# Moving two background W_down transfers to another phase and taking another seeded instruction order, in a one-core linear-attention and GeGLU block

## Chip, cores and metric

The kernel runs on one core of a Trainium2 chip. The metric is device time in microseconds (us) of that core; lower is better. A time is quoted as the median of the runs of one kernel with its lowest and highest run. All runs were fast, at a mean granted clock of 0.992 to 1.00 over the whole span.

The engines are called as the profile calls them: PE is TensorE (matmuls and transposes), PEld its weight loads, DVE VectorE, ACT ScalarE, POOL GpSimd, and SP the engine whose queue issues most loads.

## The reference

One transformer block with adaptive layer norm: linear attention, then a GeGLU feed-forward network. Shapes: x is 2048 x 1024, W_qkv 1024 x 3072, W_gate and W_up 1024 x 3584, W_down 3584 x 1024, w_mod 1024 x 6144; all bf16.

```python
mod = (silu(c) @ w_mod).reshape(1, 6, 1, -1)      # shifts, scales and gates
h = layernorm(x) * (1 + ca) + sa
q, k, v = split(h @ wqkv)                         # 32 heads of 32
pq, pk = phi(q), phi(k)                           # phi: t + 1 where t > 0, else exp(t); + 1e-6
kv = einsum('bhsd,bhse->bhde', pk, v)
z = einsum('bhsd->bhd', pk)
o = einsum('bhqd,bhde->bhqe', pq, kv) / (einsum('bhqd,bhd->bhq', pq, z) + 1e-6)
x = x + ga * (o @ wo)
h = layernorm(x) * (1 + cb) + sb
x = x + gb * ((gelu(h @ w_gate) * (h @ w_up)) @ w_down)
```

## The kernel before

Three features carry the argument. The first is how the order of instructions comes about. The kernel is not written in its final order: every call is recorded as an operation, with its predecessors, and a model of the engines then places all operations in time. PE keeps the recorded order; DVE, ACT, POOL and SP take, at each moment, the ready operation with the earliest due time. A backward sweep from the end sets the due times, a forward sweep places the operations, and this is repeated; the best forward sweep, by the model's own time, is issued. On the chip each queue then runs strictly in that order.

```python
class Plan:
    def order(self):
        best = None
        def forward(look):
            nonlocal best
            t = self.sweep(False, lambda o: (o.due, o.n), look)
            if best is None or t < best[0]:
                best = (t, sorted((op.start, op.n) for op in self.ops))
        for op in self.ops:
            op.due = op.n
        for i in range(2 * self.ROUNDS):                 # 32 rounds
            forward(i >= self.ROUNDS)
            old = [op.due for op in self.ops] if i else None
            for op in self.ops:
                op.due = op.start
            t = self.sweep(True, lambda o: (-o.due, -o.n))
            for op in self.ops:
                op.due = best[0] * (1 - op.done / max(t, best[0]))
                if old:
                    op.due += self.KEEP * (old[op.n] - op.due)
            # ... (pairs and chains keep their order)
        return [self.ops[n] for _, n in best[1]]
```

The second is a background job. The matmuls with W_down use sums of its quarters (a Strassen-like scheme). Part of these sums is made by DMA, DRAM to DRAM: a raw copy of a half of W_down into the scratch `ub`, then accumulating transfers onto it. Small marker copies on POOL hold each transfer back until PE has reached a certain instruction.

```python
def move(dst, src, add):
    gp.dma_start(out=dst, in_=src, **(dict(accum_op=ALU.add) if add else {}))

def paced_moves(seen_of, moves):
    plan.hold([op for op in plan.ops if op.eng == "PE"][-1])
    gp.tensor_copy(out=seen, in_=seen_of)                # the marker
    plan.hold(plan.ops[-1])
    for dst, src, add in moves:
        move(dst, src, add)
    plan.hold()

sums_copy = [(ub_scr[:, e], wd_v[1].rearrange("p (c e) n -> p e c n", e=2)[:, e], 0) for e in range(2)]
sums_add = [(flat[:, e, :, s, :], flat[:, f, :, t, :], 1)
            for e, s, f, t in ((0, 0, 0, 1), (0, 1, 1, 1), (1, 1, 0, 0), (1, 0, 1, 1))]
late_moves = {1: sums_copy[1:2], 3: sums_add[1:2], 5: sums_add[2:3], 7: sums_add[3:4]}

def gate_up(g):
    # ...
    for n in range(NU):                                  # units of gate/up
        # ...
        if g == 0 and n in late_moves:
            paced_moves(w["s1"][:, 0, 0, 0:1], late_moves[n])
```

The third is what the merge phase does at that time: it finishes the kv sums, makes the reciprocal denominators, writes them to DRAM and reads them back broadcast over partitions, so that DVE can multiply the queries.

```python
def merge_phase(stages):
    # ... loads of w_mod and Wo
    for i, stage in enumerate(stages):
        if i < NKB:
            kv_products(NG - 1, i)
        # ...
        if i == 5:
            den_sums(0, psN())                           # ACT: Ln, Exp; SP: write den to DRAM
        if i in (8, 10):
            den_mul(den_todo.pop(0))                     # SP: broadcast den back; DVE: multiply
        # ...

def start_phase():
    xs, loads = [], []
    for tt in range(TT):                                 # four x tiles
        xs.append(load_x(tt))
        # ...
    ca = ModRow(1, wm_ca, {0: loads[0], 2: loads[1], 4: loads[2], 6: loads[3]})   # four w_mod loads
    # ... per tile: two bn_stats, bn_aggr, rstd on ACT, normalise on DVE, eight transposes on PE
```

Of the kernel before, what the change touches and what calls it, by code (L numbers as in the profile page):

```python
# [3 lines left out]

# [19 lines left out]
class Plan:  # L24
# [115 lines left out]
    def cost(self, op, outs, ins):  # L140

        size = lambda a: math.prod(d[1] for d in a.ap[1:])
        n = max(size(a) for a in (outs if op.eng == "PE" else outs + ins))
        psum = any(a.tensor.name.startswith("psum") for a in outs + ins)
        wide = any(a.dtype == FP32 and size(a) > 8 for a in outs + ins)
        ptrs = sum(size(a) == 1 for a in ins)
        if op.eng == "PE":
            op.cost = n / 2.4 + 2.5
            op.lat = op.cost + 165
            if op.fn == "matmul" and outs[0].ap[0][1] <= 32:  # L150
                op.cost /= 3.5
        elif op.fn.startswith("dma"):
            a = outs[0]
            op.cost, op.bytes = 1000 if op.eng == "POOL" else 450, math.prod(d[1] for d in a.ap) * (4 if a.dtype == FP32 else 2)
            run = min(self.run(a) for a in outs + ins)
            if not any(a.tensor.name.startswith("mem") for a in outs + ins):
                op.bytes = int(op.bytes * self.GBPS * (12 + run / 27) / 16 / run * (2.3 if "accum_op" in op.kw else 1.6))
            op.load = a.tensor.name.startswith("mem")
            if op.fn == "dma_start_transpose":
                op.cost, op.bytes = self.transpose  # L160
            op.lat = op.cost
        elif op.eng == "ACT":
            op.cost = (55 if psum else 112) + n / 1.2 + 85 * ptrs
            op.lat = op.cost + 115
            f = op.kw.get("func")
            op.table = "g" if f == AF.Gelu_apprx_tanh else "e" if f in (AF.Exp, AF.Ln) else None
        elif op.eng == "POOL":
            op.cost = 500 if n <= 8 else 250 + n / 0.46
            op.lat = 1800 if n <= 8 else op.cost
        else:  # L170
            rate = 1.0
            if op.fn in ("tensor_scalar", "tensor_scalar_mul", "tensor_scalar_add", "tensor_copy") and not wide:
                rate = 1.0 if psum else 4.0
            elif op.fn == "tensor_tensor" and not wide:
                rate = 2.0
            op.cost = 69 + n / (0.96 * rate) + 61 * ptrs
            op.lat = op.cost + 83
# [9 lines left out]
    def sweep(self, back, key, look=False):  # L187
# [68 lines left out]
                    avail[o.eng].append(o)  # L256
        return max(op.done for op in ops)

    def order(self):


        best = None

        def forward(look):
            nonlocal best
            t = self.sweep(False, lambda o: (o.due, o.n), look)
            if best is None or t < best[0]:
                best = (t, sorted((op.start, op.n) for op in self.ops))

        for op in self.ops:  # L270
            op.due = op.n
        for i in range(2 * self.ROUNDS):
            forward(i >= self.ROUNDS)
            old = [op.due for op in self.ops] if i else None
            for op in self.ops:
                op.due = op.start
            t = self.sweep(True, lambda o: (-o.due, -o.n))
            for op in self.ops:
                op.due = best[0] * (1 - op.done / max(t, best[0]))
                if old:  # L280
                    op.due += self.KEEP * (old[op.n] - op.due)
            for a, b in [*zip(self.chain, self.chain[1:]), *self.pairs]:
                b.due = max(a.due, b.due)
        return [self.ops[n] for _, n in best[1]]

    def issue(self):
        with self.tc.manual_schedule():
# [9 lines left out]
def kernel(  # L297
# [45 lines left out]
    mem = mem_pool.tile([P, 103 * KB + KB // 2], BF16, name="mem", tag="mem")  # L343
# [51 lines left out]
    def at(off, shape, dt):  # L395
        return Ring(off, shape, dt, 1)()
# [76 lines left out]
    kvzacc = at(190, [KD, P + 1], FP32)  # L473
# [89 lines left out]
    def tt_op(out, a, b, op):  # L563
        ve.tensor_tensor(out=out, in0=a, in1=b, op=op)  # L564
# [414 lines left out]
    def kv_products(b, kb):  # L979
        glo, ghi = kb * GPB, min(KD, (kb + 1) * GPB)  # L980
        kvps = (psKV1 if b == 0 else psKV if b == 3 else QB)()[:, 0:GPB * (P + 1)].rearrange("p (g e) -> p g e", e=P + 1)
        for tl in range(TT):
            for g in range(glo, ghi):
                te.matmul(kvps[:, g - glo, :], lhsT=pks[b, tl // 2][:, tl % 2, g * P:(g + 1) * P],  # L984
                                 rhs=vta[:, tl][:, g, 0:P + 1], start=(tl == 0 and g == glo), stop=(tl == TT - 1),
                                 skip_group_check=True)
        src = kvps[:, 0:ghi - glo, :]
        if b == 0:
            ve.tensor_copy(out=kvzacc[:, glo:ghi, :], in_=src)
        else:  # L990
            tt_op(kvzacc[:, glo:ghi, :], src, kvzacc[:, glo:ghi, :], ALU.add)
# [19 lines left out]
    def den_mul(b):  # L1011
        plan.extra = 4000
        rden = rden_ring()
        plan.together(True)
        for j in range(P // DH):
            src = den_scr[b // 2][b % 2, j].rearrange("h x -> (h x)")
            sy.dma_start(out=rden[DH * j:DH * j + DH].rearrange("p g t -> p (g t)"),
                         in_=src[None, :].to_broadcast((DH, KD * TG)))
        plan.together(False)
        plan.extra = 0  # L1020
        for g in range(0, KD, 2):
            o = pqT[b][:, g:g + 2, :]
            tt_op(o, o, rden[:, g:g + 2, :], ALU.mult)
# [9 lines left out]
    def kv_diagonal():  # L1033
        gp.memset(zc, 0.0)
        for g in range(KD):
            ve.tensor_scalar_mul(out=zc[:, g, g % KH:KH * P // DH:KH], in0=maskbd[:, 0:P:DH], scalar1=kvzacc[:, g, P:P + 1])
        tt_op(KVbd, kvzacc[:, :, 0:P], maskbd[:, None, :].to_broadcast((P, KD, P)), ALU.mult)

    def kv_transposes():
        for half in range(2):  # L1040
            psk = psN(F16)[:, 0:NW].rearrange("p (g e) -> p g e", e=P)
            for g in range(4):
                te.transpose(psk[:, g, :], KVbd[:, half * 4 + g, :], ident)
            ve.tensor_copy(out=KVbdT[:, half * 4:half * 4 + 4, :], in_=psk)
# [3 lines left out]
    def move(dst, src, add):  # L1048
        gp.dma_start(out=dst, in_=src, **(dict(accum_op=ALU.add) if add else {}))  # L1049
# [13 lines left out]
    def paced_moves(seen_of, moves):  # L1063

        plan.hold([op for op in plan.ops if op.eng == "PE"][-1])
        gp.tensor_copy(out=seen, in_=seen_of)
# [5 lines that stand above are left out]
    def wd_moves(seen_of, n):  # L1072

        if wd_todo:
# [4 lines left out]
    sums_copy = [(ub_scr[:, e], wd_v[1].rearrange("p (c e) n -> p e c n", e=2)[:, e], 0) for e in range(2)]  # L1079
    flat = ub_scr.rearrange("p e c (j s n) -> p e (c j) s n", j=2, s=2)  # L1080
    sums_add = [(flat[:, e, :, s, :], flat[:, f, :, t, :], 1)
                for e, s, f, t in ((0, 0, 0, 1), (0, 1, 1, 1), (1, 1, 0, 0), (1, 0, 1, 1))]
    late_moves = {1: sums_copy[1:2], 3: sums_add[1:2], 5: sums_add[2:3], 7: sums_add[3:4]}

    def second_sum(name, f):

# [181 lines left out]
    def merge_phase(stages):  # L1268

        ms1 = ModSet(1, wm1_ring, psK)  # L1270
        sy.dma_start(out=Wo_sb, in_=A_wo.rearrange("(kd p) n -> p kd n", p=P))
        wp = list(range(KD))
        for i, stage in enumerate(stages):
            if i < NKB:
                kv_products(NG - 1, i)
            if i in (1, 3):
                for _ in range(KH):
                    ms1.step()
            if i == 3:
                kv_diagonal()  # L1280
            if i == 3 + 1:
                kv_transposes()
                ms1.columns()
                ms1.spread(0, garow, GA_SCALE)
                for g in range(KD):
                    tt_op(Wog[:, g, :], Wo_sb[:, g, :], garow, ALU.mult)
            if i == 5:
                den_sums(0, psN())
            if i in (8, 10):
                den_mul(den_todo.pop(0))  # L1290
            if i >= 6:
                wp_step(wp.pop(0))
            if i == 11:
                ms2 = ModSet(2, wm2_ring, psN)
            stage(())
        for g in wp:
            wp_step(g)
        return ms2
# [261 lines left out]
    def down_out(g):  # L1560
# [223 lines left out]
        run(*plain("t3", A22, c21_out(rest(1, 0)), False))  # L1784

    wo_phase(merge_phase(kvq_phase()))
    gate_up(0)
    down_out(0)
# [31 lines left out]
```

## Time and profile before

| | before |
|---|---|
| time, three runs before the prediction | 749.08 us (748.78 to 749.98) |
| span in the profile | 746.4 us |
| PE busy | 730.0 us (98%) |
| next busiest engine | DVE, 79% |
| PE lost beyond its pitch after 40 us | 7.27 us |
| PE lost in the start | about 10 us |

The stages in time are: start (0 to 45 us), k/v blocks (to 155), merge (to 210), output projection (to 245), gate/up 0 (to 415), down 0 (to 495), gate/up 1 (to 655), down 1. With PE at 98% a gain can come only from PE's gaps, so one reads what ended each gap. The prediction below counts these gaps by pitch, the distance of successive matmul starts in a steady stream.

A second measure is used after the result: because PE executes the same list in every kernel here (but for ten filler matmuls in two of them, which are left out), its instructions can be paired one to one between two traces, and the difference of their start times shows where one kernel runs ahead of or behind the other. I paired the weight loads, which are complete in number where a few matmul records are missing. The profiled run of before took 748.54 us.

### The profile page before, as it was taken

The numbers are of one execution on the slowest core, as the hardware profiler recorded it, in microseconds if no ns is written. First come the engines' busy times: TensorE is split into PE (matmuls) and PEld (weight loads), VectorE is DVE, ScalarE is ACT, GpSimd is POOL, SyncE is SP. The second block draws the span as 40 slices with busy tenths as digits, with TensorE's granted clock in tenths as the row PEclk, the third lists the DMA queues.
The fourth block names the chain that finished last, engine by engine and source line by source line (L and its number), as shares of the span: only waits on it lengthen the run. The fifth ranks groups of instructions, "written<-read, shape, count | busy, mean of one in ns | idle before, by whom it ended". The sixth has DMA issues, their size and how long they took to land.

```text
span 746.4 us, 11439 instructions
## 1 busy us (share of the span) xinstructions
PE 730.0 (98%) x4164; PEld 388.7 (52%) x4164; DVE 589.5 (79%) x1258; ACT 433.0 (58%) x757; POOL 95.8 (13%) x164
## 2 busy tenths in 40 slices
PE   5999999999999999999999999999999999999997
PEld 2444445444444455545454586545555555548664
DVE  6897997577786878777997888678888888888763
ACT  3665576669752768997876234027777777731000
POOL 2331245000001113342311000010000000000000
PEclk9999999999999999999999999999999999999999
DMA  8974479828899979899659799654131322399822
GB/s 298 322 212 132 152 182 163 299 101 258 245 290 257 364 253 261 259 318 227 187 191 237 210 281 314 206 183 132 60 114 57 112 73 98 110 276 302 278 104 71
DMA packets 151832, 152.79 MB, mean 205 GB/s; under 512 B 33824, under 2 KB 128544, under 8 KB 150496
## 3 DMA queue, kind: packets, MB, share of 16 engines
q1 hardware_dynamic: 128832, 122.44, 53.7%
q0 software_dynamic: 20592, 27.53, 15.6%
q10 hardware_dynamic: 2352, 2.10, 0.8%
q8 instruction: 32, 0.52, 0.3%
q14 instruction: 24, 0.20, 0.1%
HBM read 123.34 MB, written 36.04 MB: 214 GB/s over the span
## 4 chain that ended last, share of the span: by engine, by line
PE 84%; DVE 6%; ACT 5%; DMA 3%; issue 1%; SPq 1%; ACTq 0%; DVEq 0%
PE psum L1382 30%; PE psum L1588 13%; PE psum L1632 9%; PE psum L870 8%; PE psum L1393 7%; PE psum L1262 7%; PE psum L940 5%; DVE mem L564 5%; PE psum L969 4%; DMA mem<-in_A_wqkv_dram 2%; DMA mem<-in_w_mod_dram 1%; PE psum L984 1%; ACT mem L815 1%; DVE psum L564 1%; ACT psum L1436 1%
## 5 line engine op out<-in xcount | busy, mean ns | idle before, releaser
L564 DVE TENSOR_TENSOR mem<-mem 128x512 f16<-128x512 f16 (+8 forms) x669 | 307.8, 507 | 23.1 <-ACT mem L815 10.1
L1382 PE MATMUL psum<-mem 128*128 128x512 f16 x1248 | 299.1, 379 | 0.8 <-ACT psum L1436 0.5
L815 ACT ACTIVATE mem<-psum 128x256 f32<-128x256 f32 (+3 forms) x284 | 154.3, 562 | 119.9 <-PE psum L1382 45.1
L564 DVE TENSOR_TENSOR mem<-psum,mem 128x512 f16<-128x512 f32 (+4 forms) x204 | 155.4, 767 | 72.8 <-ACT mem L815 29.5
L1382 PEld LDWEIGHTS <-mem 128*128 128x128 f16 (+1 forms) x1248 | 122.0, 98 | 112.1 <-issue 2.7
L1588 PE MATMUL psum<-mem 128*128 128x512 f16 (+2 forms) x462 | 99.2, 373 | 0.5 <-DVE mem L564 0.5
L1393 PE MATMUL psum<-mem 128*128 128x256 f16 x560 | 89.5, 272 | 1.3 <-DVE psum L564 1.2
L1393 PEld LDWEIGHTS <-mem 128*128 128x128 f16 (+1 forms) x560 | 54.7, 98 | 46.8 <-issue 5.1
L1588 PEld LDWEIGHTS <-mem 128*128 128x128 f16 x462 | 45.2, 98 | 49.8 <-issue 0.7
L1632 PE MATMUL psum<-mem 128*128 128x256 f16 (+1 forms) x588 | 66.2, 273 | 0.0
L870 PE MATMUL psum<-mem 128*128 128x512 f16 (+1 forms) x280 | 62.9, 379 | 0.0
L1632 PEld LDWEIGHTS <-mem 128*128 128x128 f16 x588 | 57.5, 98 | 9.2
L1436 ACT ACTIVATE psum<-psum 128x512 f32<-128x512 f32 x56 | 32.8, 587 | 41.3 <-PE psum L1382 28.9
L1262 PE MATMUL psum<-mem 128*128 128x512 f16 x256 | 56.0, 379 | 0.0
L940 PE MATMUL psum<-mem 128*128 128x512 f16 x224 | 51.2, 379 | 0.0
L564 DVE TENSOR_TENSOR psum<-psum,mem 128x256 f32<-128x256 f32 x80 | 34.3, 429 | 17.7 <-ACT mem L815 17.3
L870 PEld LDWEIGHTS <-mem 128*128 128x128 f16 x280 | 26.9, 97 | 31.8 <-DVE mem L789 1.2
L1262 PEld LDWEIGHTS <-mem 128*128 128x128 bf16 x256 | 24.8, 98 | 30.3 <-issue 0.8
L1453 ACT ACTIVATE mem<-psum 128x512 f16<-128x512 f32 x56 | 33.1, 595 | 10.9 <-PE psum L1382 10.5
L1463 ACT ACTIVATE mem<-mem 128x512 f16<-128x512 f16 x56 | 34.9, 625 | 1.5 <-DVE mem L564 1.1
L940 PEld LDWEIGHTS <-mem 128*128 128x128 f16 (+1 forms) x224 | 21.5, 98 | 27.0 <-issue 2.0
L1049 POOL DMA_DIRECT2D ts<-in_B_w_down_dram x28 | 28.3, 1199 | 9.2 <-DMA ts<-in_B_w_down_dram 8.9
(132 smaller groups left out, 525.3 us busy)
## 6 DMA issues: line engine op xcount, KB each, us to landing
mem<-in_B_w_gate_dram SPq DMA_DIRECT2D x14, 1024.0 KB, 7.0
mem<-in_B_w_up_dram SPq DMA_DIRECT2D x14, 1024.0 KB, 5.4
mem<-in_w_mod_dram SPq DMA_DIRECT2D x24, 512.0 KB, 5.9
mem<-ts SPq DMA_DIRECT2D x6, 1792.0 KB, 6.8
mem<-in_A_x_dram SPq DMA_DIRECT2D x32, 256.0 KB, 7.7
ts<-in_B_w_down_dram POOLq DMA_DIRECT2D x28, 256.0 KB, 6.3
mem<-ub SPq DMA_DIRECT2D x16, 448.0 KB, 6.7
mem<-in_B_w_down_dram SPq DMA_DIRECT2D x12, 448.0 KB, 7.8
```

The lines of the kernel that those rows point to most:

```text
L564: ve.tensor_tensor(out=out, in0=a, in1=b, op=op)
L815: ac.activation(out=t, in_=ps, func=AF.Copy)
L870: te.matmul(ps, lhsT=A[:, k, i * P:(i + 1) * P], rhs=B[:, k, :], start=(start and k == 0), stop=(k == KH - 1), skip_group_check=True)
L940: te.matmul(o, lhsT=W[:, k, (j0 + i) * P:(j0 + i + 1) * P], rhs=h_form(a, k), start=(start and k == 0), stop=(k == KH - 1), skip_group_che ...
L1262: te.matmul(psw[:, half, :], lhsT=pqT[b][:, g, tl * P:(tl + 1) * P], rhs=Wp[:, g, half * NW:(half + 1) * NW], start=(g == 0), stop=(g == K ...
L1382: te.matmul(ps, lhsT=a[:, k, e, :], rhs=b[:, k, :], start=(start and k == 0), stop=(k == KH - 1), skip_group_check=True)
L1393: te.matmul(ps, lhsT=self.x[a][:, k, :], rhs=self.y[y][:, k, :], start=(start and k == 0), stop=(k == KH // 2 - 1), skip_group_check=True)
L1436: ac.activation(out=z, in_=x, func=AF.Copy)
L1453: ac.activation(out=o, in_=ps, func=AF.Gelu_apprx_tanh)
L1463: ac.activation(out=o, in_=o, func=AF.Gelu_apprx_tanh)
L1588: te.matmul(psm[:, q, c], lhsT=A[:, i, q * P:(q + 1) * P], rhs=wt[:, i, c], start=(start and i == 0), stop=(i == NPR - 1), skip_group_chec ...
L1632: te.matmul(ps[:, q, :], lhsT=a[:, k, q * P:(q + 1) * P], rhs=y[:, k, :], start=(start and q == 0 and k == 0), stop=(k == NPR // 2 - 1), s ...
```

## The change

The intent: free the crowded gate/up 0 of DMA traffic, by moving the second raw copy and one accumulating transfer to the merge phase, where a slice of the DMA row stood nearly idle; and find a better order by small random changes of due times, whose seeds are stored in the kernel. The model's cost of transfers was changed too.

```diff
@@ cost
-            if not any(a.tensor.name.startswith("mem") for a in outs + ins):
-                op.bytes = int(op.bytes * self.GBPS * (12 + run / 27) / 16 / run * (2.3 if "accum_op" in op.kw else 1.6))
+            dram = [a for a in outs + ins if not a.tensor.name.startswith("mem")]
+            if len(dram) == 2:
+                packet = ((10 if run == 512 else 45) + run * 0.035) * (1.7 if "accum_op" in op.kw else 1.2)
+            # ... (two more cases)
+            op.bytes = int(op.bytes * self.GBPS * packet / 16 / run)
@@ order
+    PICK, NOISE = 21, 0
+    SEEDS = (4048537842, 3052119424, ...)     # 673 seeds, cut
+    def nudge(self, seed):
+        rng = random.Random(seed)
+        at, reach = rng.random() * self.ops[-1].due, rng.choice((4e3, 10e3, 25e3))
+        size, share = rng.choice((1e3, 3e3, 8e3)), rng.choice((0.15, 0.4))
+        for op in self.ops:
+            if op.eng != "PE" and abs(op.due - at) < reach and rng.random() < share:
+                op.due += rng.gauss(0, size)
-        for i in range(2 * self.ROUNDS):
-            forward(i >= self.ROUNDS)
+        for i in range(self.PICK):
+            t = self.sweep(False, by_due, i >= self.ROUNDS)
...
-        return [self.ops[n] for _, n in best[1]]
+        for seed in self.SEEDS:
+            self.nudge(seed)
+        self.sweep(False, by_due, True)
+        return sorted(self.ops, key=lambda o: (o.start, o.n))
@@ moves
-    late_moves = {1: sums_copy[1:2], 3: sums_add[1:2], 5: sums_add[2:3], 7: sums_add[3:4]}
+    late_moves = {4: sums_add[2:3], 6: sums_add[3:4]}
@@ merge_phase
+            if i == 0:
+                paced_moves(kvzacc[:, 0, 0:1], sums_copy[1:2] + sums_add[1:2])
```

PE's instruction list is the same in both. POOL has one marker copy fewer. The other queues hold the same instructions in another order.

## The prediction

> **What bounds the kernel now.** I read the page first (busy shares and slices), then a table of busy time by stage, then the waits of TensorE, then short stretches of the timeline around each gap. The page:
>
> ```profile
> PE 730.0 (98%) x4164; PEld 388.7 (52%) x4164; DVE 589.5 (79%) x1258; ACT 433.0 (58%) x757; POOL 95.8 (13%) x164
> PEclk9999999999999999999999999999999999999999
> DMA  8974479828899979899659799654131322399822
> ```
>
> TensorE (PE) is busy for 730.0 of the 746.4 us span at the full granted clock, and no other engine is over 79%. The last line is the busy share of the DMA engines in 40 slices of 18.7 us: the ninth digit (149 to 168 us) is 2, while the slices 13 to 22 of gate/up 0 (245 to 415 us) are mostly 8 and 9. The table by stage, with columns PE, weight load, DVE, ACT, POOL, clock, DMA share, GB/s (start; k/v blocks; merge; output projection; gate/up 0; down 0; gate/up 1; down 1):
>
> ```profile
> 0.00:45.00 45.00, 35.30 (x212) 16.11 (x213) 35.73 (x105) 21.84 (x39) 10.79 (x38) 1.00 0.92 302
> 45.00:155.00 110.00, 109.98 (x595) 53.06 (x594) 88.78 (x176) 70.88 (x86) 31.96 (x51) 1.00 0.70 184
> 155.00:210.00 55.00, 54.43 (x336) 23.96 (x334) 41.80 (x73) 41.47 (x60) 0.31 (x1) 1.00 0.69 208
> ...
> 245.00:415.00 170.00, 168.74 (x868) 84.62 (x867) 140.37 (x327) 133.35 (x250) 45.00 (x63) 1.00 0.89 254
> 415.00:495.00 80.00, 80.00 (x518) 50.50 (x517) 63.03 (x112) 19.52 (x30) 4.38 (x6) 1.00 0.84 250
> 495.00:655.00 160.00, 159.10 (x915) 89.25 (x914) 133.41 (x326) 117.20 (x242) 1.45 (x2) 1.00 0.31 98
> ```
>
> Idle TensorE time sits in the start (9.7 us) and the tail; the stage that the change relieves, gate/up 0, has 170.00 - 168.74 = 1.26 us of it although its DMA share is 0.89. The waits of TensorE over the whole run name no DMA after the start:
>
> ```profile
> PE psum L676 <- DVE mem L663: 5.5, 1, 5.5
> PE psum L713 <- DMA mem<-in_c_dram: 2.2, 1, 2.2
> PE psum L1393 <- DVE psum L564: 1.2, 4, 0.4
> PE psum L636 <- DMA mem<-in_w_mod_dram: 1.0, 2, 0.7
> PE psum L691 <- DVE mem L684: 0.7, 1, 0.7
> PE psum L999 <- DVE mem L564: 0.5, 1, 0.5
> PE psum L1588 <- DVE mem L564: 0.5, 1, 0.5
> PE psum L1382 <- ACT psum L1436: 0.5, 2, 0.3
> ```
>
> The columns are total us, times, longest. The two DMA rows lie before 28.1 us. The rest are short waits for DVE or ACT. One stands for all, at 321 us of gate/up 0; TensorE and then ACT:
>
> ```profile
> 320.65 1.03 PE L1382 MATMUL psum<-mem 128*128 128x512 f16 x4
> 321.99 0.81 PE L1382 MATMUL psum<-mem 128*128 128x512 f16 x3 [0.31 <-ACT psum L1436]
> ```
>
> ```profile
> 319.18 1.05 ACT L1218 ACTIVATE mem<-mem 128x1024 bf16<-128x1024 bf16 x1
> 320.13 0.19 ACT L1218 ACTIVATION_READ_ACCUMULATOR mem<-mem 128x1 f32 x1
> 320.22 1.23 ACT L1225 ACTIVATE mem<-mem 128x1024 f16<-128x1024 bf16 x1
> 321.36 0.58 ACT L1436 ACTIVATE psum<-psum 128x512 f32<-128x512 f32 x1
> ```
>
> ACT ran a 1.05 us and a 1.23 us piece of the late layer norm, which nobody needs soon, just ahead of the 0.58 us PSUM copy that TensorE needs.
>
> **The trace counted by pitch.** In steady streams the starts of consecutive matmuls are 216 ns apart at 512 columns and 109 ns at 256. Four of the first kind take 0.864 us, so the matmul at 321.99 could have begun at 320.65 + 0.86 = 321.51: it lost 0.48 us, not the 0.31 shown as idle, since an isolated matmul's bar (379 ns) hides part of the gap. I took every start-to-start distance of the trace against the pitch of its width, and summed what exceeds it by more than 60 ns outside the packed 32-column matmuls, whose gaps (93 to 258 ns) repeat whatever the order:
> - before 40 us: about 10 us, of which 5.68 is the first transpose's wait for the normalised first tile and 1.06 a wait for a modulation weight load;
> - at 75 us, before a k block, on DVE: 0.50; at 108, 146 and 163 us: 0.41;
> - at 193.3 us, denominator sums, on DVE: 0.84, of which some 0.15 stays in any order, so 0.69;
> - gate/up 0: 0.255 x4 + 0.477 + 0.325 + 0.579 + 0.066 + 0.073 = 2.54, mostly on the PSUM copy of ACT;
> - gate/up 1: 0.390 + 0.226 + 0.427 + 0.504 + 0.085 + 0.086 on DVE's PSUM add, and six of 0.122 on an ACT copy, 2.45;
> - at 740.5 us: 0.68, the two halves of the last output bank, which take turns in one PSUM bank.
> After 40 us these are 7.27 us. The other 720.3 us are pitch.
>
> **What the Trainium skill says.** (1) "TensorE: Matmul & The Clock Gate", section "Wait — 56ns, not 53.3ns?", gives warm start-to-start times of N / 2.4 GHz plus about 2.5 ns, 215.7 ns for 512 columns. The trace agrees: 40 matmuls in 8.63 us from 245.75 us, 216 ns each. So no reordering can press this part. (2) The same page's table of specifications gives ScalarE and VectorE queues that are strictly first in, first out. The 321 us stretch agrees: the PSUM copy ran 0.58 us late behind work of no urgency. (3) "Trainium Kernel Development and Optimization", section "Key Constraints", says that DMAs of the SP, ACT and POOL queues share the same 16 engines. That would let the W_down moves slow the weight loads of gate/up 0; the trace has the 0.89 share, but no wait of TensorE for a load there.
>
> **The change part by part.** (a) The moves. The second raw copy of W_down (1792 KB, DRAM to DRAM) and one of the accumulating transfers (896 KB) leave gate/up 0, where POOL issued them at 253.46 and 283.37 us, and go behind the first kv product of the merge phase; the other two accumulating ones go from units 5 and 7 to units 4 and 6. No bytes are added. POOL loses two small marker copies and gains one. TensorE does not wait for POOL or for these bytes: their first reader issues at 394 us and TensorE meets down 0 without a gap at 415. Direct worth: 0 us. Relief of contention: no load was waited for, so also 0, at most a few tenths through DVE's weight sums starting earlier. Cost in the merge phase: it falls next to the nearly idle slice and near the loads of Wo and w_mod; I count 0. (b) The order. TensorE's sequence is the same in both programs, all 8330 rows (matmuls and weight loads); DVE, ACT, POOL and SP are reordered nearly everywhere. So the sum of pitches stays, and only the listed stalls can go or grow. Comparing places: of the six ACT copies that stalled in gate/up 0, two or three have lost the long norm piece or the late eviction ahead of them, one stands as it did, and one (the sixteenth of all) now has a 1.23 us norm piece directly in front that it had not. I take half of 2.54 back: -1.2. In gate/up 1, of the four DVE adds that lost 0.2 to 0.5, three now have only short work or a PSUM eviction before them, while one keeps a pattern that cost 0.39 elsewhere; -1.0 of 2.45. Denominator sums and the k block: half of 0.69 + 0.50, -0.6. The end stays. (c) The start. SP now issues the first x tile ahead of c; an issue takes about 0.45 us there, so the first statistics begin some 0.45 us sooner. But DVE does six statistics instead of five, 0.69 us each, before it normalises tile 0, and the last of the four modulation loads keeps its place in the queue, so the stretch that waits for it (to 12.9 us) stays: -0.1. The sum is -1.2 - 1.0 - 0.6 - 0.1 = -2.9 us: 749.08 - 2.9 = 746.2 us.
>
> **The rivals.** *New stalls take the place of old ones.* The order comes from a model, and many of its seeds can be fitted to the model and not to the chip; gate/up has ACT at 133.35 of 170 us and DVE at 140.37, little room. For: the long norm piece before the sixteenth copy. Then 748.5 to 750. *The contention was real though hidden*, weight loads landing late and shifting all of DVE's order; then gate/up 0 loses nearly all its stalls and the start gains, about 743. Against: DVE waits there for ACT and TensorE, not for loads. *The moves collide in the merge phase*: DMA shares of 0.8 to 0.9 follow in 168 to 205 us, and a late denominator broadcast would hold DVE (2.1 us of waiting for it in all now); then +1 to +2, near 748.
>
> **Range and chances.** The time before spread from 748.78 to 749.98. A recovery of all 7.27 would give 741.8, which no reordering reaches; nothing recovered gives 749. I put 8 in 10 on 743.3 to 749.0, with 746.2 the middle. A gain over 2% needs 15 us, more than all stalls after 40 us and half of the start together: 1%. A loss over 2% needs a new wait of 15 us that nothing announces: 1%. Within 2%: 98%.
>
> **What would show it.** Right: PE busy time falls together with the span (gaps below an isolated matmul's 163 ns of fill count as busy), clock 1.00, the same matmul counts, stalls by pitch in both gate/up stages near 1.3 and 1.4 us, TensorE's first transpose still near 7.5 to 8 us, DMA share in the merge window up from 0.69 and in gate/up 0 down from 0.89. Wrong: a TensorE wait for a load in 155 to 245 us; or a transpose that starts much earlier and a start that ends over 1 us sooner; or a gain in gate/up 0 that the ACT order does not explain. The weakest steps are the halves taken in (b), which rest on order alone.

## The result, and the profile after

| | before | after |
|---|---|---|
| median of 4 runs | 749.46 us (748.78 to 749.98) | 745.75 us (744.92 to 747.56) |
| ratio | | 0.9954, 95% interval 0.9934 to 0.9975 |

A ratio in this document is the record's: fast runs of one kernel over fast runs of the other from the same rounds, so not quite the ratio of the medians quoted. The gain is 3.7 us by the medians; 2.9 were predicted, and 745.75 lies within the range. The run that was profiled is the slowest of the four, 747.56; that matters below.

The busy shares of the changed kernel, from its page (14 matmul records are missing, so 728.9 is slightly low):

```profile
PE 728.9 (98%) x4150; PEld 389.2 (52%) x4164; DVE 592.3 (79%) x1258; ACT 433.1 (58%) x757; POOL 94.7 (13%) x163
```

Its busy time by stage (columns PE, weight load, DVE, ACT, POOL, clock, DMA share, GB/s), for the start, merge, gate/up 0 and gate/up 1:

```profile
0.00:45.00 45.00, 34.05 (x195) 14.96 (x198) 32.69 (x99) 20.43 (x36) 12.76 (x41) 1.00 0.87 285
...
155.00:210.00 55.00, 54.43 (x348) 24.40 (x345) 42.98 (x75) 43.66 (x60) 3.73 (x4) 1.00 0.92 239
...
245.00:415.00 170.00, 169.56 (x875) 85.45 (x874) 142.19 (x326) 135.69 (x254) 39.09 (x59) 1.00 0.87 246
...
495.00:655.00 160.00, 160.00 (x925) 90.27 (x923) 134.99 (x332) 117.32 (x243) 1.43 (x2) 1.00 0.33 102
```

Against the table of before, PE's idle time fell from 1.26 to 0.44 us in gate/up 0 and from 0.90 to 0 in gate/up 1. The DMA share went from 0.69 to 0.92 in the merge phase, but in gate/up 0 only from 0.89 to 0.87. The start, however, has more idle time (10.95 us against 9.70), and PE has done fewer weight loads by 45 us (198 against 213). The largest waits of PE in the whole run:

```profile
PE psum L784 <- DVE mem L771: 6.4, 2, 5.2
PE psum L821 <- DMA mem<-in_c_dram: 3.6, 1, 3.6
...
PE psum L1503 <- DVE psum L672: 0.3, 1, 0.3
```

The ACT copy of before (0.5 us, twice) and most of the 1.2 us on DVE's PSUM add are gone from this list. What is new is the second wait in the first row, for the normalised second tile. By pitch, the stalls left are 0.255 x2 + 0.424 = 0.93 us in gate/up 0 (2.54 before) and 0.090 + 0.156 + 0.123 x2 + 0.135 = 0.63 us in gate/up 1; 0.68 us at the end, as before. For gate/up 1 the prediction lists 2.45 us before the change, but the trace of before has seven stalls of 0.122 us on the ACT copy there and not six, so it was 2.57.

Here is the copy of the 321 us stretch, the fourteenth of its line, in the changed kernel, with the matmuls around it. No norm piece stands before it any more, and PE runs on:

```profile
323.67 0.58 ACT L1546 ACTIVATE psum<-psum 128x512 f32<-128x512 f32 x1 [0.97 <-PE psum L1503]
```

```profile
323.47 4.70 PE L1492 MATMUL psum<-mem 128*128 128x512 f16 x21
```

**The start.** DVE of the changed kernel, with idle time and its releaser in brackets:

```profile
8.43 0.49 DVE L771 TENSOR_SCALAR mem<-mem 128x1024 f16<-128x1024 bf16 x1
11.26 0.69 DVE L750 BATCH_NORM_STATS2 mem<-mem 128x6 f32<-128x512 bf16 x1 [2.33 <-DMA mem<-in_A_x_dram]
11.87 0.53 DVE L771 TENSOR_SCALAR mem<-mem 128x1024 f16<-128x1024 bf16 x1
```

And of before:

```profile
7.33 0.49 DVE L663 TENSOR_SCALAR mem<-mem 128x1024 f16<-128x1024 bf16 x1
7.73 0.69 DVE L642 BATCH_NORM_STATS2 mem<-mem 128x6 f32<-128x512 bf16 x1
8.34 0.53 DVE L663 TENSOR_SCALAR mem<-mem 128x1024 f16<-128x1024 bf16 x1
```

In both the second normalisation follows a statistic. In the changed kernel it is the first half of the fourth x tile's, whose load SP issues behind two loads of w_mod; it waits 2.33 us for that load, and the second tile, which was ready, waits behind it. PE gets the second tile's transposes at 12.46 instead of 9.82 us. The consequence lies a little later, in the first plain v matmuls (changed kernel, then before):

```profile
17.69 5.55 PE L799 MATMUL psum<-mem 128*128 128x512 f16 x16 [0.65 <-DVE mem L792]
```

```profile
15.03 4.18 PE L691 MATMUL psum<-mem 128*128 128x512 f16 x16 [0.66 <-DVE mem L684]
```

The same sixteen matmuls take 5.55 us instead of 4.18. Until 21.7 us they start 427 ns apart, then 216: the array ran at half clock until then, and only until 12.3 us in before. The Trainium skill, "TensorE: Matmul & The Clock Gate", section "What's actually happening", says that the array is at 1.2 GHz by default and goes to 2.4 GHz after a window of about 3.4 us of sustained work, and that this window is not tied to the kernel's start. 427 against 216 ns agrees.

The traces show more, worked out from their clock switches and matmul bars. In order_only, fix_warm and start_old, three experiments below, the later switches lie 86, 58 and 11 periods of 3.413 us after the first full clock. Cut into windows of that length, the changed kernel has PE idle for 1.34, 1.04 and 0.65 us in the three windows from 8.0 to 18.2 us, all of which left it at half clock, and for 0 us in the window that ends at 21.7. Before has 0 us in the window from 8.9 to 12.3. Over all fourteen traces, by their bars, full clock followed each half-clock window with up to 0.61 us of idle PE and none with 0.64 or more. So several short waits in the start can hold back the clock, and the wait for the fourth x tile, to 12.46 us, is one of them; that it alone did so in this run is not shown.

The position of PE against before (us, negative is ahead), as the amount gained or lost in each part:

| profile of | to 30 us | 30 to 245 | gate/up 0 | gate/up 1 | at 740 us |
|---|---|---|---|---|---|
| after | +3.1 | -0.5 | -1.6 | -1.95 | -1.0 |

The columns leave out the stretches between the parts, in which nothing moved by over 0.1 us. The gate/up stages gain 3.6 us, more than the 2.2 predicted, and this profiled run loses 3.1 in the start. Of these 3.1, 2.65 us are there at 13 us already, 1.4 are added by 20 us at half clock, and 0.9 come back by 30. Its three unprofiled sisters were about 2 us faster. Whether the start costs 3 us always, and whether the moves earn any of the gain, was left to experiments.

### The profile page after: what moved, and what is told of

The parts are those of the page before. It is cut to its first block, busy times and chain, and to the rows that moved or that the text cites. A ratio compares the mean times of both kernels' runs of the same rounds, so it can differ in the third digit from the quotient of the medians.

```text
span 745.4 us, 11428 instructions
## 1 busy us (share of the span) xinstructions
PE 728.9 (98%) x4150; PEld 389.2 (52%) x4164; DVE 592.3 (79%) x1258; ACT 433.1 (58%) x757; POOL 94.7 (13%) x163
## 4 chain that ended last, share of the span: by engine, by line
PE 91%; DMA 6%; DVE 2%; issue 1%; SPq 0%; ACT 0%; DVEq 0%
PE psum L1492 34%; PE psum L1698 13%; PE psum L1742 9%; PE psum L1503 8%; PE psum L978 8%; PE psum L1370 6%; PE psum L1048 5%; PE psum L1077 4%; PE psum L799 2%; DMA mem<-in_A_x_dram 2%; DMA mem<-den 1%; DMA mem<-in_w_mod_dram 1%; DMA mem<-in_B_w_gate_dram 1%; PE psum L1092 1%; DVE mem L672 1%
## 5 line engine op out<-in xcount | busy, mean ns | idle before, releaser
L672 DVE TENSOR_TENSOR mem<-mem 128x512 f16<-128x512 f16 (+9 forms) x669 | 310.3, 505 | 31.9 <-ACT mem L923 11.9
L923 ACT ACTIVATE mem<-psum 128x512 f16<-128x512 f32 (+3 forms) x284 | 154.1, 563 | 111.0 <-PE psum L1742 39.8
L672 DVE TENSOR_TENSOR psum<-psum,mem 128x256 f32<-128x256 f32 x80 | 34.2, 428 | 15.1 <-ACT mem L923 14.5
L1157 POOL DMA_DIRECT2D ts<-in_B_w_down_dram x28 | 31.2, 1455 | 8.9 <-DMA ts<-in_B_w_down_dram 8.5
```

The costliest lines, as they stand in the source:

```text
L672: ve.tensor_tensor(out=out, in0=a, in1=b, op=op)
L923: ac.activation(out=t, in_=ps, func=AF.Copy)
```

## The experiments

Theories at the outset. **Order**: the gain is the order of DVE and ACT, most of it in gate/up, and the moves are free and worth nothing (the prediction). **Moves**: the moves relieve gate/up 0. **Start**: the new order in front costs about 3 us, which putting back the old one would return.

To edit the order alone, the search was replaced by a stored list of operation numbers. With the list that the search itself gives, this builds the identical program. Each experiment then changes that list:

```diff
     def order(self):
-        # ... 21 rounds of sweeps, 673 nudges, the last sweep
-        return sorted(self.ops, key=lambda o: (o.start, o.n))
+        return [self.ops[n] for n in STORED]
```

In the diffs below a line stands for an engine's sequence in that list. PE's is the same in all but warm and fix_warm, which add ten matmuls. All kernels gave the correct result.

### First group: the parts apart

The kernel before took 749.17 us in this group (11 runs, 748.06 to 749.98).

**The moves alone (moves_only).**

```diff
-DVE, ACT, SP, POOL: changed order
+DVE, ACT, SP, POOL: order of before; the moved transfers and their markers at their new places on POOL
```

> The transfers moved as in the change, every other instruction in the order of the kernel before. Theory 1 (the order carries the gain, the moves nothing): within 0.5 us of the kernel before, near 749.5 us, and the stalls of gate/up 0 and 1 by pitch still near 2.5 us each. Rival (the moves relieve gate/up 0 of hidden contention): 1.5 us or more below the kernel before, near 747.5, with fewer stalls in gate/up 0 alone.

Measured: 752.04 us (750.27 to 753.41), ratio 1.0044 (1.0031 to 1.0057). This was a miss: under the old order the moves cost about 3 us. In its profile nothing is gained in gate/up 0 (the change of position over that stage is 0.0), and 2.3 us are lost before it, in the merge phase (155 to 210 us). DVE's wait for the denominators in the merge phase, in before and then in moves_only:

```profile
DVE mem L564 <- DMA mem<-den: 2.1, 1, 2.1
```

```profile
DVE mem L593 <- DMA mem<-den: 7.1, 2, 3.9
```

Here the accumulating transfer is in flight from 162.6 to 174.7 us. The busy table of the end of that stretch (DMA share and GB/s last; a share over 1 means that the recorded times of packets overlap on an engine), before and moves_only:

```profile
170.00:174.00 4.00, 4.00 (x21) 1.77 (x19) 3.31 (x6) 4.00 (x5) 0.00 (x0) 1.00 0.44 142
```

```profile
170.00:174.00 4.00, 4.00 (x21) 1.80 (x19) 3.62 (x6) 4.00 (x6) 0.00 (x0) 1.00 1.32 244
```

From 165 to 170 us the DMA share is 0.64 in before and 1.16 in moves_only. The write of the denominators and two w_mod loads are issued in these nine microseconds. From the issue of that write to the issue of the broadcast 5.7 us pass in before (168.30 to 174.00) and 6.6 in moves_only (167.61 to 174.18), and the broadcast then takes 7.2 us to land instead of 4.9. DVE's and PE's reaction:

```profile
185.72 2.50 DVE L593 TENSOR_TENSOR mem<-mem 128x1024 bf16<-128x1024 bf16 x4 [3.19 <-DMA mem<-den]
```

```profile
186.47 3.71 PE L1291 MATMUL psum<-mem 128*128 128x512 f16 x14 [1.12 <-DVE mem L593]
```

The 3 us are shown by the timed rounds, and so is their cause in the edit, since nothing but the place of the transfers and their markers differs. The profiled run is the fastest of the five, at a clock of 1.00; three of the other four list 0.997 or 0.998, which in the profiles of order_only and fix_warm below is one stretch of half clock. What was lost in those runs no trace shows. How the delay is passed on is less certain too: the broadcast begins only 0.5 us before the accumulating transfer lands, so it is slowed less by that transfer itself than, as I read it, by the loads that it held up. This is the third rival of the prediction, and it came true for this combination.

**The order alone (order_only).**

```diff
-late_moves = {4: sums_add[2:3], 6: sums_add[3:4]}          # and two moves in the merge phase
+late_moves = {1: sums_copy[1:2], 3: sums_add[1:2], 5: sums_add[2:3], 7: sums_add[3:4]}
 DVE, ACT, SP: changed order
-POOL: changed order
+POOL: changed order, the transfers and markers of before at their old places
```

> The order of the changed kernel on every engine, with the four late transfers back in gate/up units 1, 3, 5 and 7. Theory 1: as the changed kernel, 745 to 746.5 us, 3 to 4.5 us below the kernel before. Rival (contention): at least 1.5 us above the changed kernel, near 747.5.

Measured: 750.15 us (747.82 to 751.73), ratio 1.0015 (0.9999 to 1.0031). Also a miss: no gain is left, and the rival's direction is right. Gate/up 1 still gains 1.96 us, but gate/up 0 loses 3.1. There DVE, and behind it PE, stood still:

```profile
306.36 0.29 DVE L614 TENSOR_TENSOR mem<-mem 128x256 f16<-128x256 bf16 x1 [6.83 <-DMA mem<-in_B_w_gate_dram]
```

```profile
307.31 1.86 PE L1432 MATMUL psum<-mem 128*128 128x512 f16 x4 [2.92 <-DVE mem L614]
```

DVE, in its fixed order, waits 6.83 us for a load of W_gate; PE idles 2.92 us. From 306.9 to 310.3 us PE's pitch is doubled, which costs another half of 3.4 us. The sum, 2.9 + 1.7 less the gain of about 1.9, is 2.7; 3.1 was measured. The stage's row shows both, a clock of 0.99 and a DMA share of 0.91:

```profile
245.00:415.00 170.00, 166.47 (x853) 83.63 (x852) 138.78 (x321) 131.55 (x248) 43.76 (x63) 0.99 0.91 253
```

So the old transfers in gate/up 0 do harm a load there, under the new order. In before's own profile no wait of PE or DVE there showed it. The load was issued at 292.5 us and DVE went on at 306.4, 13.8 us later; in gateup_new, below, the same load took 6.3. One of the accumulating transfers was in flight from 288.5 to 302.7 us. In before it went from 283.4 to 296.6, so the new order of POOL also issues it 5 us later, and it overlaps the load for longer. The trace is one run, but four of the other five list a clock of 0.998 as it does, and the one at 1.00 is the fastest, 747.82 us. That the transfers delayed the load is inferred from what was put back and from this overlap.

**The old start (start_old).**

```diff
-DVE, ACT, SP, POOL: changed order
+DVE, ACT, SP, POOL: order of before up to the last plain v matmul (about 30 us), then the rest in the changed order
```

> The changed kernel, but every engine's instructions up to the last value projection of the start (about 30 us) in the order of the kernel before. Theory 1 (the new start costs 1 to 3 us: the profiled run of the changed kernel is 2.9 us behind at 31 us, then gains 3.9 us): 742 to 744.5 us, TensorE's clock granted in full from about 12 us, first transpose near 7.9 us. Rival (the new start is as good, and the 2.9 us in the profile are chance of that one run): 745.7 us, as the changed kernel.

Measured: 753.35 us (751.29 to 754.93), ratio 1.0057 (1.0041 to 1.0072), a miss. To 30 us it is where expected (0.3 us ahead of before instead of 3.1 behind), but at the seam it breaks:

```profile
43.20 1.29 DVE L700 BATCH_NORM_STATS2 mem<-mem 128x6 f32<-128x512 bf16 x2 [6.89 <-DMA mem<-in_A_x_dram]
```

An x tile of the next block lands too late for a statistic that stands early in DVE's queue; PE stalls 5.2 us and runs at half clock from 51.3 to 54.7 us. As I read it, this is an artefact of the splice, whose two sides do not agree on which loads are under way, and it says nothing of the start's cost. A finer edit was needed.

**The order from gate/up on (gateup_new).**

```diff
-DVE, ACT, SP, POOL: changed order
+DVE, ACT, SP, POOL: as moves_only up to the first gate/up matmul, then the rest in the changed order
```

> The order of the kernel before, with the moves, up to the first gate/up matmul; the order of the changed kernel from there. Theory 1 (gate/up 0 and 1 give 1.6 and 1.9 us in the profiles, before them the order gives only 0.5): 3 to 3.7 us below the kernel before, near 746. Rival (the gain is spread, the k/v and merge order has a share over 1 us): over 747.

Measured: 747.16 us (746.26 to 749.32), ratio 0.9981 (0.9967 to 0.9996), over the 746 expected and just over the rival's 747: the expectation had taken the moves to be free. By position it gains 2.02 us in gate/up 0 and 1.97 in gate/up 1, and loses 2.5 us in the merge phase, as moves_only does. It isolates the gain: the order in the two gate/up stages, with the moves gone from there, is worth 4.0 us in the profile, and 4.9 by the medians against moves_only. Beside the changed kernel it also shows that the new order before gate/up is what avoids the moves' cost; in this sense the rival is right. This holds in the profiles without filler matmuls; the two with them (warm and fix_warm, below) have the new order there and lose 3.1 and 5.4 us before gate/up.

### Second group: the start, and the clock

Before: 748.69 us (747.77 to 752.25). The changed kernel was run again as a control (after2), with no edit.

> The changed kernel again, its order written down as a list in place of the search; the control of this group. The theory from the traces so far: 745 to 746.5 us, and a new profile some 3.5 us shorter than that of the kernel before, since in the first profile of the changed kernel the clock of TensorE was granted in full only at 21.7 us (12.3 in the kernel before, 13.3 in the run with the new order and the old transfers), which cost that run alone about 2 us. Rival (the new start always costs 3 us): the same late clock and the same 2.9 us behind at 31 us.

Measured: 746.38 us (745.63 to 747.26), ratio 0.9965 (0.9948 to 0.9981). In this profile PE is 0.1 us ahead of before at 30 us, not 3.1 behind. The fourth x tile's statistic waits here too, but shorter, and the clock was full from 13.5 us:

```profile
9.98 0.69 DVE L701 BATCH_NORM_STATS2 mem<-mem 128x6 f32<-128x512 bf16 x1 [1.11 <-DMA mem<-in_A_x_dram]
```

So the 3.1 us were one run's, the first profiled one. But this run lost elsewhere: 2.3 us at 241 and 258, behind three waits of DVE for x tiles, two in the output projection and one in the first gate/up unit, of which before has none.

```profile
DVE mem L623 <- DMA mem<-in_A_x_dram: 6.1, 3, 3.1
```

**The old start, finely (start_fix).**

```diff
 SP, the first 12 loads:
-x0, c, x1, x2, w_mod 1, w_mod 0, x3, w_mod 2, w_mod 3, W_v ...
+c, x0, x1, x2, x3, w_mod 0, w_mod 1, w_mod 2, w_mod 3, W_v ...
 DVE, the first 26 instructions, and ACT, the first 11: the same instructions
-in the changed order
+in the order of before (tile 1 normalised ahead of any statistic of the fourth tile)
 everything else: changed order
```

> The changed kernel with its own first instructions of SP (12 loads), DVE (26) and ACT (11) put in the relative order of the kernel before; nothing else is spliced. If the new start typically costs 0.3 us and now and then 2 to 3: median 0.3 to 1 us below the control and no run above 746.5. If it always costs 3 us: 742.5 to 743. If it costs nothing: as the control.

Measured: 744.55 us (743.22 to 745.98), ratio 0.994 (0.9921 to 0.996). This is 1.8 us under after2 of the same rounds, more than the 0.3 to 1 expected. PE is 0.3 us ahead of before at 30 us, 0.2 better than after2; most of the rest of the difference between the two profiles goes with the waits for x tiles, 0.7 us in all here and 6.1 there. So the start itself is worth a few tenths, with more in some runs, and how the later part follows from it is open.

**Filler matmuls (warm, fix_warm).** If the clock's late grant costs time, early work on PE should bring it forward.

```diff
         te.transpose(pcc, c8[0:KD, :], identb[0:KD, :])
+        keep_warm(10, NW)
```

warm is the changed kernel with this line, fix_warm is start_fix with it.

> The changed kernel with ten filler matmuls of 512 columns behind the first transpose, in TensorE's idle time from 3.7 to 8.9 us. If the late clock is what makes some runs slow: full clock from 7 to 11 us in the profile, median 0 to 1 us below the control, spread of the runs under 1.5 us. If fillers delay the first transposes: above the control.

Measured: 748.33 us (746.57 to 751.26), ratio 0.9996 (0.9973 to 1.002): a loss of 2 us against after2 by the medians, and a miss. In its profile full clock comes at 16.5 us, later and not earlier, and the start is 2.2 us behind before: now the first tile's statistic already waits.

```profile
7.36 0.70 DVE L701 BATCH_NORM_STATS2 mem<-mem 128x6 f32<-128x512 bf16 x1 [2.27 <-DMA mem<-in_A_x_dram]
```

> Both: the old relative order of the first instructions and the ten fillers. If the two add: 744 to 745 us, the fastest of the group; if the start is bound by the modulation loads whatever the order: as the control, 745.5.

Measured: 745.74 us (743.29 to 749.73), ratio 0.9961 (0.9933 to 0.9989), about the control and not the sum of the two. Full clock came at 9.4 us, the earliest of all, and the position at 30 us is +0.1 against before, so the earlier clock bought nothing by then. The profiled run is the slowest of them: DVE waited 6.2 us for a denominator broadcast in the merge phase, and PE lost 5.4 us between 30 and 245 us. One stall there, 2.46 us up to 207.5, was followed by half clock until 210.8. The spread is too wide for a verdict. Why ten matmuls that read only constants go with late x tiles was not settled.

### Third group: smaller steps, on another chip

Before: 749.74 us (747.6 to 751.07). start_fix was run again as a control (start_fix2, no edit against start_fix).

> The kernel of start_fix again, unchanged, as the control of this group: 743.5 to 745.5 us. A median over 746 would say that its gain of 1.8 us over the changed kernel was chance.

Measured: 744.1 us (743.27 to 746.43), ratio 0.9936 (0.9916 to 0.9956), as on the first chip (0.994) and as expected. PE is busy 169.76 of 170 us in gate/up 0 and all of 160 in gate/up 1.

**Only the loads of the start (start_sp).**

```diff
 SP, the first 12 loads:
-x0, c, x1, x2, w_mod 1, w_mod 0, x3, w_mod 2, w_mod 3, W_v ...
+c, x0, x1, x2, x3, w_mod 0, w_mod 1, w_mod 2, w_mod 3, W_v ...
 DVE, ACT, POOL: changed order
```

> The changed kernel with the first 12 loads of SP alone in the old order (c ahead of the first x tile, all four x tiles ahead of the modulation weights); DVE and ACT stay new. If the late fourth x tile in front of the in-order DVE is the cause: within 0.5 us of start_fix. If DVE's own order is: within 0.5 us of the changed kernel, 746.

Measured: 745.37 us (744.84 to 746.75), ratio 0.9949 (0.9932 to 0.9966). The wait of the fourth tile's statistic is gone:

```profile
9.16 0.69 DVE L701 BATCH_NORM_STATS2 mem<-mem 128x6 f32<-128x512 bf16 x1
```

This settles the cause of that wait: with DVE's order untouched, x3's earlier issue alone removes it. The time lies between after2's and start_fix2's ratios (0.9965, 0.9936), and its interval touches both, so neither expectation is met within its 0.5 us.

**The raw copy earlier (early_copy, moves_early).** If the raw copy pushes the accumulating transfer onto the denominators, issuing it earlier should help.

```diff
 POOL:
-kv product 0 of the merge phase, marker, raw copy, accumulating transfer
+first norm of the last k/v block (about 85 us), raw copy ... kv product 0, marker, accumulating transfer
```

early_copy is start_fix with this, moves_early is moves_only with this.

> start_fix with the second raw copy of W_down issued behind the first norm of the last k/v block, at about 85 us where the DMA engines idle, so that only the accumulating transfer stays in the merge phase and lands by about 166 us. If the moved transfers make the denominator broadcasts late: DVE's wait for them back from 3.8 to about 2 us, and 0 to 1 us below start_fix with a smaller spread. If the copy at 85 us delays the transposes of that block: above it.

Measured: 743.56 us (742.73 to 745.04), ratio 0.9924 (0.9907 to 0.9942). The best time of all, but only 0.5 us under start_fix2 of the same rounds, with overlapping intervals. The merge phase has a DMA share of 0.86 where start_fix2 has 0.96, but the denominator wait in the profile is 3.4 us (start_fix: 3.8), so the expected fall to 2 did not come.

> moves_only with the same earlier copy. If its loss of 3.3 us is the two transfers running into the denominator broadcasts: 749 to 750 us, the loss mostly gone. If the loss comes from something else in the moves (POOL's markers, gate/up): 751.5 to 752.5 as before.

Measured: 750.87 us (748.53 to 752.03), ratio 1.0017 (0.9997 to 1.0037), against 1.0044 for moves_only in another group. By the ratios 0.44% of loss became 0.17%, across two groups; the time lies between the two expectations. The profile still has DVE waiting 2.3 + 3.9 us for denominators, and the accumulating transfer still landed at 174.2 us, where the broadcasts begin. It hardly went earlier: POOL, in its fixed order, stands before it at a memset that waits for PE.

```profile
161.19 0.31 POOL L1064 MEMSET mem<- 128x256 f16 x1 [6.82 <-PE psum L611]
161.67 1.93 POOL L1079 DMA_DIRECT2D ub<-ub  x1 [0.17 <-issue]
```

It is issued at 161.7 us here and at 162.6 in moves_only; in early_copy at 160.9, landing at 171.7 and not at the 166 expected. So these two runs took the raw copy out of the merge phase but left the accumulating transfer nearly where it was, and the raw copy is not the only cause.

### All profiles in one table

Gain or loss of PE against the profile of before, in us; the last column is the position at 740 us.

| kernel | median | to 30 us | 30 to 245 | gate/up 0 | gate/up 1 | at 740 us |
|---|---|---|---|---|---|---|
| after | 745.75 | +3.1 | -0.5 | -1.6 | -1.95 | -1.0 |
| after2 | 746.38 | -0.1 | +0.3 | +0.2 | -1.9 | -1.5 |
| moves_only | 752.04 | -0.7 | +2.5 | 0.0 | 0.0 | +1.7 |
| order_only | 750.15 | +0.3 | -0.7 | +3.1 | -2.0 | +0.7 |
| start_old | 753.35 | -0.3 | +7.1 | -1.7 | -2.0 | +3.1 |
| gateup_new | 747.16 | -0.4 | +2.5 | -2.0 | -2.0 | -1.95 |
| start_fix | 744.55 | -0.3 | -0.6 | -1.9 | -1.95 | -4.8 |
| warm | 748.33 | +2.2 | +3.1 | -0.9 | -2.0 | +2.5 |
| fix_warm | 745.74 | +0.1 | +5.4 | -2.0 | -2.0 | +1.5 |
| start_fix2 | 744.10 | -0.4 | -0.5 | -2.0 | -2.0 | -4.9 |
| start_sp | 745.37 | +0.1 | -0.7 | -0.9 | -2.0 | -3.5 |
| early_copy | 743.56 | -0.2 | -0.6 | -2.0 | -2.0 | -4.8 |
| moves_early | 750.87 | +0.2 | +3.3 | 0.0 | 0.0 | +3.4 |

The pattern: gate/up 1 gains 1.9 to 2.0 us in every kernel with the new order there and nothing in the two with the old one. Gate/up 0 gains 1.6 to 2.0 where the new order has the moves gone from there; after2, warm and start_sp keep less, because PE waits for a late DVE at the stage's beginning, for 1.6, 0.8 and 0.6 us. DVE waits for two x tiles in the output projection in many of these runs, up to 3.6 us, without a loss here; these three have a third such wait, of 1.1 to 2.1 us, at 256 to 262 us. Each row is a single profiled run, and so is before, so its last column need not match the median.

## Why the prediction was right or wrong

The time was right: 3.7 us of gain by the medians where 2.9 was predicted, inside the range and within 2%. The sum came out for reasons that are only partly the predicted ones.

**Gate/up 0 (-1.2 predicted).** The mechanism held: stalls behind work without urgency disappear, and the order of DVE and ACT does it, since the moves alone leave the stage at 0.0. The size was too small: -1.6 to -2.0 where nothing else stalls the stage. The step that fell short is "half of 2.54"; 0.93 us was left, not 1.3. One named place was wrong: the sixteenth ACT copy does have the long norm piece before it, but PE did not feel it. ACT and PE of the changed kernel:

```profile
334.41 1.23 ACT L1333 ACTIVATE mem<-mem 128x1024 f16<-128x1024 bf16 x1
```

```profile
335.56 0.58 ACT L1546 ACTIVATE psum<-psum 128x512 f32<-128x512 f32 x1
```

```profile
335.36 2.97 PE L1492 MATMUL psum<-mem 128*128 128x512 f16 x13
```

Thirteen matmuls run through the copy's start without a break. What stands directly in front of an instruction is not the cost; when the consumer needs it is.

**Gate/up 1 (-1.0 predicted).** Same mechanism, and the prediction has half the size: -1.95 in eleven profiles, 0.63 us left of 2.57 (the prediction's 2.45 misses one of the seven ACT-copy stalls).

**Denominator sums and k block (-0.6 predicted).** In the profiles free of other trouble the middle gains 0.5 to 0.7. The size holds, by luck. By the paired positions of the changed kernel both stalls went whole and not by half, -0.5 us at the k block of 75 us and -0.9 at the denominator sums of 193 us, and +0.7 came in anew at 177 to 181 us of its trace. Order_only has this new stall too and moves_only has not, so it belongs to the order: the first rival, in one place.

**The start (-0.1 predicted).** Wrong in sign. The prediction named the two changes in the queues (first x tile ahead of c; six statistics before the first normalisation) but not the one that mattered: x3's load behind two w_mod loads, with its statistic ahead of the second tile's normalisation. Start_sp shows that this load order makes the wait. At 30 us the profiles with DVE's new start stand at -0.1 to +0.3 us against before (after2, order_only, start_sp), those with the old start at -0.7 to +0.2: a cost of a few tenths at most, as the two ranges overlap. In the first profile of the changed kernel, where the half clock lasted until 21.7 us, it was 3.1 us. The first transpose, foretold near 7.5 to 8 us, began at 8.98 there.

**The moves (0 predicted, both as relief and as cost).** The sum is near zero for the change as a whole, but not because each part is. Alone they cost about 3 us, in the profile by late denominators (the third rival, put at +1 to +2). Without them the new order loses 3.1 us in gate/up 0 behind a late W_gate load (the second rival). The prediction's argument, "no load was waited for", was true of the old order, and said nothing of the new one. The two parts fit together only as a pair: their separate effects, +2.9 us (moves_only) and +1.0 us (order_only) against before in that group, add up to +3.9, and the pair gives -2.3 to -3.7. The new order has the moves' wait too, but hides it: DVE waits 3.9 us for denominators in the changed kernel, and PE is busy 54.43 us of the merge stage, exactly as in before. And it needs the W_gate load on time, which the transfers in their old place delayed.

**What would have shown it wrong.** The DMA share in the merge phase rose as foretold (0.69 to 0.92), and that in gate/up 0 fell, by 0.02. Neither number showed whether anyone waits.

**Slips in the recorded text.** The 0.58 us by which the copy at 321 us is said to have run late is its own duration; what PE lost is the 0.48 of the count by pitch. The 720.3 us of pitch do not follow from the numbers given (746.4 - 10 - 7.27 is 729), and the page counts 4164 matmuls and 4164 weight loads, 8328 and not 8330. No step rests on these.

**Open.** Of the 1.8 us between start_fix and after2, 0.2 to 0.3 are seen at 30 us. The rest goes with x tiles that come late at 234 to 258 us in after2 and not in start_fix, and no experiment separates chance from cause there. Why the filler matmuls hurt is open too, and so is whether early_copy's 0.5 us is real.

## What to carry to other kernels

With fixed, in-order queues a late DMA becomes a stall of everything behind it, so an order and the transfers beside it are good or bad only together: test them apart to understand them, but keep or drop them as a pair. When a searched order is accepted, look at its start on the chip, several times, because its cost can be tenths in one run and three microseconds in the next, as here, where the run with the longer wait for a load also came late to full clock. A long stall of PE can cost more than itself: after the stalls of 2.46, 2.92 and 5.2 us in fix_warm, order_only and start_old PE ran at half clock until 3.4 us after the clock had dropped, and after the longest of the others past the start, 2.13 us in warm, it did not.

## What the Trainium skill lacked or had wrong

- "TensorE: Matmul & The Clock Gate", section "What's actually happening": it puts the fall to half clock after an idle window of about 3.4 us. Here a wait of 2.92 us (order_only) was already followed by half clock from 306.9 to 310.3 us, and one of 2.46 us (fix_warm) by half clock from 207.3 to 210.8; the 3.413 us before these two switches still held 0.9 and 1.1 us of matmuls, so the window need not be idle throughout. In moves_early 1.40 us of idle time in a window was enough (11.7 to 15.1 us), while 1.60 at 244 us was not, so idle time as the profile shows it is not the whole rule. The length of the slow period, 3.4 us, agrees, and so does the pitch of 427 against 216 ns. The profile's own row of clock digits hides this at the start: it shows 9 in all slices though the pitch was 427 ns until 21.7 us.
- The same page, section "Back-to-back issue gap": it gives about 131 ns per matmul at 512 columns as a sustained rate, and calls N / 2.4 + 2.5 the gap of an isolated one. In this kernel's sustained streams the pitch is 216 ns, in the profiles of before and after alike, which is what this formula gives (215.8).
- The same page's advice to warm the clock up with matmuls is for benchmarks. Here ten early filler matmuls gave 748.33 us against 746.38 without; why is open.
- No page that I read gives durations of accumulating DRAM-to-DRAM transfers. Here 896 KB took 9.8 to 14.0 us from issue to landing in the merge phase, and the raw copy of 1792 KB, which changes the type as it goes, 8.0 to 9.5.
